# Linear attention and a gated mixture product on one Trainium2 core: VectorE's reciprocals and x multiplications queued behind the features of later pairs

## The chip, the core and the metric

The kernel runs on one core of a Trainium2 chip. Times are device microseconds (us) of one execution; the figure of a kernel is the median of its runs. The engines are TensorE (PE in the views, with its weight loads as PEld), VectorE (DVE), ScalarE (ACT), GpSimd (POOL) and SyncE (SP), which issues all DMA transfers of this kernel. Each engine works through its own instruction queue in order.

## The reference

```python
def phi(x):
    proj = x @ w_phi                                   # 64 -> 128 features
    proj = proj - max(abs(proj), axis=-1)
    return concatenate([exp(proj), exp(-proj)])        # 256
q_p, k_p = phi(q), phi(k)
kv = k_p.T @ v                                         # per batch and head
z = sum(k_p over tokens)
num, den = q_p @ kv, q_p @ z + 1e-6
x = (num / den), heads side by side                    # 4608 tokens x 512
out = ((x @ w_a) * (x @ w_b)) @ w_out                  # 512 -> 1536 -> 512
```

8 batches, 8 heads, 576 tokens, head size 64; all in float32.

## The kernel before

**Attention** goes over 32 pairs of heads (4 for each of 8 batches). For one pair, K is projected to features in two halves of two token chunks (`features`: TensorE makes pk, VectorE takes the maximum m, L228, and subtracts it into kd, L229; ScalarE takes the exponentials), a remainder chunk is shared by two pairs, and K's features are multiplied with V into kv. The query side makes e0 and e1, and `numerators` multiplies them with kv: the numerators go to DRAM as xun, the denominators as den. `reciprocals` loads the denominators back in another layout (r, 128 x 9), adds EPS (L394), takes the reciprocal (L395) and stores it as rec in DRAM.

**The mixture** works on blocks of 512 tokens; blocks 0 to 8 of the first pass, with 4 of 12 slices of the inner 1536 columns, run beside attention. `x_chunk` loads 128 rows of the numerators (x32) and the reciprocals, spread over 64 rows each (rb, two buffers), and VectorE multiplies them (L583). `load_x` splits the result into xh and xl, and `moe_block` makes, for each of four slices, pa and pb on TensorE (L626, 24 matmuls), h = pa * pb on VectorE (L631), its split hh and hl, and at the end the output product po (L647, 48 matmuls): 144 matmuls a block. Blocks 7 and 8 need the last batch and run after attention, beside the decoding of the weights of the second pass (`decode`, L453 to L459, `load_factors`), whose matmuls (`winograd`, L721) follow block 8. Chunk c of block j needs pair 4b + c, where b is the batch that holds the block's last token.

**Order.** `attention_steps` plans every step of a pair at a turn (4 turns from pair to pair after the first 7, 5 before); steps are traced turn by turn, and between the turns `run` traces steps of the mixture at PACE steps a turn. That is program order. The scheduler then fixes each engine's order with a time model of its own: an instruction goes when its inputs are ready by that model, the earliest in program order first. So instructions whose inputs the model takes for ready can go ahead of earlier ones. A block's multiplications, traced when its four pairs are long done, thus stand one by one in VectorE's queue, each soon after its own pair's reciprocal. The chip keeps the order, whatever the real arrival times are.

Of the kernel before, what the change touches and what calls it, by code (L numbers as in the profile page):

```python
# [13 lines left out]
ALU = mybir.AluOpType  # L14
# [4 lines left out]
P = 128  # L19
EPS = 1e-6  # L20


TURNS0, TURNS, PAIRS0 = 5, 4, 7
# [7 lines left out]
Q_TURNS, Q_STEP, NUM_TURN, QB, PB, Q32 = (4, 6), 2, 12, 2, 2, 3  # L31


DECODE_TURN, X_LAG, BLOCK_LAG = 2, 2, 8
PACE0, PACE, PACE0_UNTIL = 0.6, 0.62, 18


# [22 lines left out]
def tile_kernel(ctx, tc, qT, km, kr, vm, vr, w_phi, w_a, w_b, w_out, out):  # L60
# [13 lines left out]
    nc = tc.nc  # L74
    B, H, _, S = qT.shape
    NPAIR = H // 2
    D, F = w_phi.shape
# [29 lines left out]
    def products(a, b):  # L107

        if len(a) == 1:
            return [(a[0], b[0])]  # L110
        return [(a[0], b[0]), (a[0], b[1]), (a[1], b[0])]
# [32 lines left out]
    def engine(step, b):  # L144
        return {"v": nc.vector, "s": nc.scalar}[ENGINES[step][min(b, 2)]]
# [7 lines left out]
    def split(hi, lo, src, eng_hi, eng_lo):  # L153

        copy(eng_hi, hi, src)
        eng_lo.tensor_tensor(lo, src, hi, op=ALU.subtract)  # L156

    def stack(hi_lo, src, eng_hi, eng_lo):

        copy(eng_hi, hi_lo, src)  # L160
        eng_lo.tensor_tensor(hi_lo[D:], src[D:], hi_lo[D:], op=ALU.subtract)

    def k_load(b, pr, a1, a2, ps, consts, st):
        vaug = consts[-1]
        u = f"{b}_{pr}"
        i = b * NPAIR + pr
        n = NFULL * P
        k32 = a1.tile([P, n], F32, tag="k32", bufs=2, name=f"k32_{u}")
        nc.sync.dma_start(k32, km[b, pr])
        if i < PLAIN_KV:  # L170
            v32 = a1.tile([P, NFULL, 2, D + 1], F32, tag="vl", bufs=2, name=f"v32_{u}")
            nc.vector.memset(v32[:, :, :, D : D + 1], 1.0)
        else:
            v32 = a1.tile([P, NFULL, 2, D], F32, tag="v32", name=f"v32_{u}")
        nc.sync.dma_start(v32[:, :, :, :D], vm[b, pr])
        yield
        st["k", b, pr] = (k32,)
        if i >= PLAIN_K:
            kh, kl = (a1.tile([P, n], F32R, tag=f"k{p}", bufs=2, name=f"k{p}_{u}") for p in "hl")
            split(kh, kl, k32, engine("k_hi", b), engine("k_lo", b))  # L180
            st["k", b, pr] = (kh, kl)
        yield
        st["v", b, pr] = (v32,)
        if i >= PLAIN_KV:
            va = vaug[pr % 2]
            vl = a1.tile([P, NFULL, 2, D + 1], F32R, tag="vl", bufs=2, name=f"vl_{u}")
            split(va[:, :, :, :D], vl[:, :, :, :D], v32, engine("v_hi", b), engine("v_lo", b))
            st["v", b, pr] = (va, vl)
        yield
# [25 lines left out]
    def features(u, i, k_, c0, n, a2, ps, consts):  # L215

        wk32, wks = consts[3:5]
        d = a2.tile([P, 4, F], F32, tag="kd", bufs=2, name=f"kd_{u}")[:, : 2 * n]
        pk = ps.tile([P, 2, 2 * F], F32, tag="att", name=f"pk_{u}")
        parts = products(k_, (wk32,) if len(k_) == 1 else wks)  # L220
        for c in range(n):
            tok = slice((c0 + c) * P, (c0 + c + 1) * P)
            for n_, (x_, w_) in enumerate(parts):
                at = dict(start=(c == n_ == 0), stop=(n_ == len(parts) - 1))
                nc.tensor.matmul(pk[:, c], x_[:, tok], w_, skip_group_check=True, **at)
        p = pk[:, :n].rearrange("p c (j f) -> p (c j) f", j=2)
        m = a2.tile([P, 4], F32, tag="m", name=f"m_{u}")
        nc.vector.tensor_reduce(out=m[:, : 2 * n], in_=p, op=ALU.max, axis=AX.X, apply_absolute_value=True)  # L228
        nc.vector.tensor_tensor(d, p, m[:, : 2 * n].unsqueeze(2).broadcast_to([P, 2 * n, F]), op=ALU.subtract)  # L229
        yield  # L230
        plain = i < PLAIN_KV
        shape = [P, 2 * n, 2, F]
        if plain:
            e = a2.tile(shape, F32, tag=f"keh{n}", bufs=n, name=f"ke_{u}")
        else:
            e = a2.tile([P, 4, 2, F], F32, tag="ke", bufs=2, name=f"ke_{u}")[:, : 2 * n]
        nc.scalar.activation(e[:, :, 0, :], d, AF.Exp)  # L237
        nc.scalar.activation(e[:, :, 1, :], d, AF.Exp, scale=-1.0)
        es = (e,)
        if not plain:  # L240
            eh = a2.tile(shape, F32R, tag=f"keh{n}", bufs=n, name=f"keh_{u}")
            el = a2.tile(shape, F32R, tag=f"kel{n}", bufs=n, name=f"kel_{u}")
            split(eh, el, e, engine("ke_hi", i // NPAIR), nc.vector)
            es = (eh, el)
        yield es
# [16 lines left out]
    def rest_chunk(b, g, a1, a2, ps, consts, st):  # L262

        gen = features(f"{b}_{g}_r", b * NPAIR + 2 * g, st["rk", b, g], 0, 1, a2, ps, consts)
        yield next(gen)
        st["re", b, g] = next(gen)
        yield
# [121 lines left out]
    def reciprocals(b, pr, a1):  # L389
        n = 2 * S // P  # L390
        hs = slice(2 * pr, 2 * pr + 2)
        r = a1.tile([P, n], F32, tag="rec", bufs=2, name=f"r_{b}_{pr}")
        nc.sync.dma_start(r, den[b][hs].rearrange("h (a n) -> (h a) n", n=n))
        nc.vector.tensor_scalar_add(r, r, EPS)  # L394
        nc.vector.reciprocal(r, r)  # L395
        nc.sync.dma_start(rec[b][hs].rearrange("h (a n) -> (h a) n", n=n), r)
        yield

    def attention_steps(pools, consts, st):

        stages, x_first = [], first_block_x()

        def plan(unit, turns):
            for t in turns:
                stages.append((t, len(stages), unit))

        for i in range(B * NPAIR):
            b, pr = divmod(i, NPAIR)
            t0 = TURNS0 * min(i, PAIRS0) + TURNS * max(i - PAIRS0, 0)
            plan(k_load(b, pr, *pools, consts, st), [t0 + t for t in LOAD_TURNS])  # L410
            if pr % 2 == 0:
                plan(rest_load(b, pr // 2, *pools, consts, st), [t0 + t for t in REST_LOAD_TURNS])
            for c0 in range(0, NFULL, 2):
                plan(k_chunks(b, pr, c0, *pools, consts, st), [t0 + K_STEP * c0 // 2 + t for t in K_TURNS])
            if pr % 2 == 0:
                plan(rest_chunk(b, pr // 2, *pools, consts, st), [t0 + t for t in REST_TURNS])
            plan(rest_add(b, pr, st), [t0 + REST_ADD_TURNS[pr % 2]])
            plan(k_finish(b, pr, *pools, consts, st), [t0 + t for t in KV_TURNS])
            plan(q_project(b, pr, *pools, consts, st), [t0 + t for t in PROJECT_TURNS])
            for j in range(2):  # L420
                plan(q_side(b, pr, j, *pools, consts, st), [t0 + Q_STEP * j + t for t in Q_TURNS])
            plan(numerators(b, pr, *pools, consts, st), [t0 + NUM_TURN])
            plan(reciprocals(b, pr, pools[0]), [t0 + NUM_TURN])
            if b == 0:
                plan(x_first, [t0 + NUM_TURN + X_LAG])
            if pr == NPAIR - 1:
                plan(b, [t0 + NUM_TURN])
        stages.sort(key=lambda x: x[:2])
        for turn, group in itertools.groupby(stages, key=lambda x: x[0]):
            ready = None  # L430
            for _, _, unit in group:
                if isinstance(unit, int):
                    ready = unit
                else:
                    next(unit, None)
            yield turn, ready
# [130 lines left out]
    def x_chunk(j, c, pool):  # L567

        T, u = TS[0], f"0_{j}"
        x32 = pool.tile([P, T], F32, tag="x32", bufs=NCC, name=f"x32_{u}_{c}")  # L570
        rb = pool.tile([P, T], F32, tag="rb", bufs=2, name=f"rb_{u}_{c}")

        t = j * T
        while t < (j + 1) * T:
            b, s0 = divmod(t, S)
            n = min(S - s0, (j + 1) * T - t)
            src, dst = slice(s0, s0 + n), slice(t - j * T, t - j * T + n)
            nc.sync.dma_start(x32[:, dst], xun[b][c * P : (c + 1) * P, src])
            for i in range(2):
                h = 2 * c + i  # L580
                nc.sync.dma_start(rb[i * D : (i + 1) * D, dst], rec[b][h : h + 1, src].broadcast_to([D, n]))
            t += n
        nc.vector.tensor_tensor(x32, x32, rb, op=ALU.mult)  # L583
        return x32

    def load_x(j, pool):
# [6 lines left out]
    def first_block_x():  # L593

        for x_ in load_x(0, xpool):
            first_x.append(x_)
            yield
# [404 lines left out]
    with ExitStack() as c:  # L1002
        pools = attention_pools(c)
# [129 lines left out]
```

## Time and profile before

| | |
|---|---|
| median of 3 runs | 1243.63 us (1243.04 to 1245.67) |
| the profiled execution, whole time | 1245.73 us |
| its span, first to last instruction | 1243.9 us |
| TensorE busy | 1193.5 us (96%) |
| VectorE busy | 1003.8 us (81%) |
| ScalarE busy | 631.7 us (51%) |
| mean granted TensorE clock | 0.995 |

A busy share is a mean over stages: attention with the mixture blocks fills the first half of the span, the second and third pass of the mixture the rest. A matmul's end is modelled, so its shown duration (about 0.4 us for 512 columns) overlaps the next ones; the step from start to start is the pace.

### The profile page before, as it was taken

The numbers are of one execution on the slowest core, as the hardware profiler recorded it, in microseconds if no ns is written. First come the engines' busy times: TensorE is split into PE (matmuls) and PEld (weight loads), VectorE is DVE, ScalarE is ACT, GpSimd is POOL, SyncE is SP. The second block draws the span as 40 slices with busy tenths as digits, with TensorE's granted clock in tenths as the row PEclk, the third lists the DMA queues.
The fourth block names the chain that finished last, engine by engine and source line by source line (L and its number), as shares of the span: only waits on it lengthen the run. The fifth ranks groups of instructions, "written<-read, shape, count | busy, mean of one in ns | idle before, by whom it ended". The sixth has DMA issues, their size and how long they took to land.

```text
span 1243.9 us, 18463 instructions
## 1 busy us (share of the span) xinstructions
PE 1193.5 (96%) x6533; PEld 935.6 (75%) x6533; DVE 1003.8 (81%) x1715; ACT 631.7 (51%) x1236; POOL 159.4 (13%) x68
## 2 busy tenths in 40 slices
PE   7888999999999999989999999999999999999997
PEld 4455767776777777777678888878788888888887
DVE  6999978787887979866398865888897688888686
ACT  5756756665665656746254444343444243434332
POOL 2332223231332313312000000000000000000000
PEclk9999999999999999999999999999999999999999
DMA  6665444453442535422373241747489714241312
GB/s 206 192 198 164 123 139 135 120 160 104 152 145 90 172 102 158 133 75 99 97 249 115 98 122 32 242 153 244 152 296 387 250 51 152 68 157 64 127 69 84
DMA packets 129788, 182.84 MB, mean 147 GB/s; under 512 B 35488, under 2 KB 64672, under 8 KB 129696
## 3 DMA queue, kind: packets, MB, share of 16 engines
q1 hardware_dynamic: 129696, 181.67, 45.5%
q8 instruction: 51, 0.84, 0.3%
q14 instruction: 41, 0.34, 0.1%
HBM read 123.06 MB, written 58.56 MB: 146 GB/s over the span
## 4 chain that ended last, share of the span: by engine, by line
PE 44%; DVE 27%; DMA 20%; issue 4%; ACT 3%; SPq 2%; DVEq 0%; ACTq 0%
PE pba L721 6%; PE paa L721 6%; PE po L933 5%; PE po L647 4%; PE pb L626 4%; DMA rb<-rec 4%; PE poa L826 3%; PE pa L626 3%; DMA rec<-r 3%; PE pac L721 3%; PE pbc L721 3%; DMA r<-den 2%; DVE qs L338 2%; PE kvps L281 2%; DVE kel L156 2%
## 5 line engine op out<-in xcount | busy, mean ns | idle before, releaser
L351 POOL PARTITION_ALL_REDUCE mb<-p x64 | 159.2, 2507 | 424.3 <-ACT p L344 330.5
L355 ACT ACTIVATE qe<-p 128x576 f32<-128x576 f32 x64 | 44.0, 687 | 60.4 <-DVE p L352 46.1
L371 PE MATMUL pn<-qe,kvh 128*64 128x288 f32 x512 | 71.9, 414 | 1.4 <-ACT qe L355 0.8
L156 DVE TENSOR_TENSOR kel<-ke,keh 128x1024 fp32r<-128x1024 f32 x50 | 63.0, 1262 | 9.3 <-ACT keh L149 9.0
L237 ACT ACTIVATE ke<-kd 128x512 f32<-128x512 f32 x64 | 40.6, 634 | 50.2 <-DVE kd L229 49.6
L626 PE MATMUL pb<-xh,w_b_h 128*128 128x512 f32 x144 | 58.6, 407 | 7.5 <-DVE h L631 6.8
L647 PE MATMUL po<-hh,w_o_h 128*128 128x512 f32 x144 | 57.6, 407 | 5.2 <-DVE h L631 4.4
L647 PE MATMUL po<-hl,w_o_h 128*128 128x512 f32 x144 | 57.8, 403 | 1.8 <-DVE hl L156 1.7
L626 PE MATMUL pa<-xh,w_a_h 128*128 128x512 f32 x144 | 57.6, 400 | 1.6 <-DVE xh L151 1.5
L149 ACT CAST hh<-h 128x512 fp32r<-128x512 f32 x36 | 22.4, 622 | 72.4 <-DVE h L631 72.3
L626 PE MATMUL pa<-xl,w_a_h 128*128 128x512 f32 x144 | 57.3, 398 | 1.1 <-DVE xl L156 1.1
L583 DVE TENSOR_TENSOR x<-x,rb 128x512 f32<-128x512 f32 x36 | 25.9, 719 | 40.1 <-DMA rb<-rec 37.2
L626 PE MATMUL pb<-xl,w_b_h 128*128 128x512 f32 x144 | 57.5, 399 | 0.0
L626 PE MATMUL pb<-xh,w_b_l 128*128 128x512 f32 x144 | 57.3, 398 | 0.0
L647 PE MATMUL po<-hh,w_o_l 128*128 128x512 f32 x144 | 57.1, 398 | 0.0
L281 PE MATMUL kvps<-keh,vaug 128*65 128x256 f32 x200 | 56.6, 283 | 0.5 <-ACT keh L149 0.4
L626 PE MATMUL pa<-xh,w_a_l 128*128 128x512 f32 x144 | 56.9, 395 | 0.0
L371 PEld LDWEIGHTS pn<-qe,kvh 128*64 128x64 f32 x512 | 34.4, 136 | 29.8 <-issue 5.5
L933 PE MATMUL po<-hl,w_o_h 128*128 128x512 f32 x144 | 56.3, 391 | 0.0
L281 PE MATMUL kvps<-kel,vaug 128*65 128x256 f32 x200 | 56.2, 281 | 0.0
L281 PE MATMUL kvps<-keh,vl 128*64 128x256 f32 x200 | 56.1, 280 | 0.0
L933 PE MATMUL po<-hh,w_o_l 128*128 128x512 f32 x144 | 56.1, 389 | 0.0
(331 smaller groups left out, 3689.3 us busy)
## 6 DMA issues: line engine op xcount, KB each, us to landing
x<-xnorm SPq DMA_DIRECT2D x32, 512.0 KB
o<-part SPq DMA_DIRECT2D x61, 256.0 KB
q<-in_qT SPq DMA_DIRECT2D x108, 144.0 KB
xun<-xn SPq DMA_DIRECT2D x32, 288.0 KB
xnorm<-x SPq DMA_DIRECT2D x36, 256.0 KB
part<-o SPq DMA_DIRECT2D x18, 512.0 KB
part<-o SPq DMA_DIRECT2D x36, 256.0 KB
k<-in_km SPq DMA_DIRECT2D x32, 256.0 KB
```

Of the source, the lines that this page charges most:

```text
L156: eng_lo.tensor_tensor(lo, src, hi, op=ALU.subtract)
L237: nc.scalar.activation(e[:, :, 0, :], d, AF.Exp)
L281: nc.tensor.matmul(st["kv_ps", b, pr][:width, j], v_[:, j, :width], e_[:, j], start=(left == NFULL and j == 0 and n_ == 0), stop=(left == ...
L351: nc.gpsimd.partition_all_reduce(mb, p32, P, bass_isa.ReduceOp.absmax)
L355: nc.scalar.activation(e[:, 0], p32, AF.Exp)
L371: nc.tensor.matmul(pn[j * D : (j + 1) * D, :HALF], kv[:, 2 * j + s, :D], e[:, s, tok], **at)
L583: nc.vector.tensor_tensor(x32, x32, rb, op=ALU.mult)
L626: nc.tensor.matmul(acc, w[:, cc * P : (cc + 1) * P], x, start=(k == 0), stop=(k == 3 * NCC - 1))
L647: nc.tensor.matmul(acc, w[:, cc * P : (cc + 1) * P], h, start=(k == 0), stop=(k == 3 * NFS[p] - 1))
L721: nc.tensor.matmul(accs[to][i], w_, x_, skip_group_check=True, **at)
L826: nc.tensor.matmul(accs[to][m], w_, x_, skip_group_check=True, **flags)
L933: nc.tensor.matmul(acc[key], w[:, cc * P : (cc + 1) * P], h[:, tok], skip_group_check=True, **n_)
```

## The change

Two kinds of VectorE instructions get edges that set their place in VectorE's queue, without a wait on any result. The addition in front of the reciprocal of pair i goes behind the subtraction kd of pair i + 3, second half. The multiplication of chunk c of a block goes behind the kd of pair + 4, first half, where pair is the one that the chunk needs last. Only kd from pair 7 on are used. Where there are no four later pairs (blocks 7 and 8), the multiplication is kept behind the VectorE instruction traced just before it. In program order, the addition is traced three turns after the denominators' reload, and the first block's x one turn later.

```diff
-DECODE_TURN, X_LAG, BLOCK_LAG = 2, 2, 8
+DECODE_TURN, X_LAG, BLOCK_LAG = 2, 3, 8
...
+    behind = {}
+
+    def placed(i, c0, op):
+
+        if i >= PAIRS0 and (i + c0[0], c0[1]) in behind:
+            with tc.issue_after(behind[i + c0[0], c0[1]]):
+                return op()
+        return op()
...
-        nc.vector.tensor_tensor(d, p, m[:, : 2 * n].unsqueeze(2).broadcast_to([P, 2 * n, F]), op=ALU.subtract)
+        kd = nc.vector.tensor_tensor(d, p, m[:, : 2 * n].unsqueeze(2).broadcast_to([P, 2 * n, F]), op=ALU.subtract)
+        if n == 2:
+            behind[i, c0] = kd.ins
...
         nc.sync.dma_start(r, den[b][hs].rearrange("h (a n) -> (h a) n", n=n))
-        nc.vector.tensor_scalar_add(r, r, EPS)
+        yield
+        placed(b * NPAIR + pr, (3, 2), lambda: nc.vector.tensor_scalar_add(r, r, EPS))
         nc.vector.reciprocal(r, r)
...
-            plan(reciprocals(b, pr, pools[0]), [t0 + NUM_TURN])
+            plan(reciprocals(b, pr, pools[0]), [t0 + NUM_TURN + t for t in (0, 3)])
...
-        nc.vector.tensor_tensor(x32, x32, rb, op=ALU.mult)
+        multiply = lambda: nc.vector.tensor_tensor(x32, x32, rb, op=ALU.mult)
+        pair = ((j + 1) * T - 1) // S * NPAIR + c
+        if pair + 4 < B * NPAIR:
+            placed(pair, (4, 0), multiply)
+        else:
+            tc.keep_in_program_order(multiply())
         return x32
```

## Rows read from the trace of the kernel before

**Rows 1.** Windows: us from:to, length, then busy us of each engine.

```profile
core 0: us, PE busy (x) PEld busy (x) DVE busy (x) ACT busy (x) POOL busy (x), PEclk, DMA share, GB/s
165.00:575.00 410.00, 392.42 (x2577) 301.54 (x2576) 338.10 (x534) 253.88 (x522) 108.92 (x42) 0.99 0.42 128
```

**Rows 2.** Groups by line, VectorE, 165 to 575 us: busy, mean ns, idle before.

```profile
L583 DVE TENSOR_TENSOR x<-x,rb 128x512 f32<-128x512 f32 x21 | 15.6, 744 | 30.3 <-DMA rb<-rec 27.9 <-issue 2.3
L394 DVE TENSOR_SCALAR r<-r 128x9 f32<-128x9 f32 x22 | 4.8, 220 | 32.7 <-DMA r<-den 32.7
```

**Rows 3.** The page's chain that ended last, shares by engine.

```profile
PE 44%; DVE 27%; DMA 20%; issue 4%; ACT 3%; SPq 2%; DVEq 0%; ACTq 0%
```

**Rows 4.** Waits of TensorE, 165 to 575 us: us in total, times, longest.

```profile
PE pb L626 <- DVE h L631: 6.8, 5, 2.4
PE po L647 <- DVE h L631: 3.5, 1, 3.5
PE pq L343 <- DVE qs L338: 3.4, 2, 1.9
PE po L647 <- DVE hl L156: 1.7, 3, 0.6
PE pa L626 <- DVE xh L151: 1.3, 1, 1.3
PE pq L343 <- DVE rkh L151: 0.6, 1, 0.6
```

**Rows 5.** Timeline of VectorE, 297 to 320 us: start, length, idle time before.

```profile
297.92 0.17 DVE L394 TENSOR_SCALAR r<-r 128x9 f32<-128x9 f32 x1 [2.31 <-DMA r<-den]
...
303.04 0.69 DVE L583 TENSOR_TENSOR x<-x,rb 128x512 f32<-128x512 f32 x1 [4.70 <-DMA rb<-rec]
303.65 0.69 DVE L631 TENSOR_TENSOR h<-pb,h 128x512 f32<-128x512 f32 x1
...
307.52 0.68 DVE L229 TENSOR_TENSOR kd<-pk,m 128x512 f32<-128x512 f32 x1
...
319.66 0.69 DVE L229 TENSOR_TENSOR kd<-pk,m 128x512 f32<-128x512 f32 x1
```

**Rows 6.** Timeline of TensorE around the same stall.

```profile
302.05 0.28 PE L281 MATMUL kvps<-keh,vaug 128*65 128x256 f32 x1
304.39 0.50 PE L626 MATMUL pb<-xh,w_b_h 128*128 128x512 f32 x1 [2.07 <-DVE h L631]
```

**Rows 7.** Windows where the granted clock (PEclk) falls, and right after.

```profile
460.30:463.70 3.40, 3.19 (x8) 2.52 (x9) 3.40 (x7) 1.10 (x2) 0.00 (x0) 0.50 0.36 135
463.70:467.10 3.40, 3.40 (x23) 2.78 (x23) 3.37 (x8) 2.73 (x5) 0.00 (x0) 1.00 0.42 117
552.45:555.86 3.41, 3.41 (x12) 2.65 (x12) 3.38 (x6) 3.41 (x8) 0.00 (x0) 0.50 0.64 210
```

**Rows 8.** Timeline of SP's queue, 298 to 301 us.

```profile
298.37 0.32 SPq L396 DMA_DIRECT2D rec<-r  x1
299.77 1.12 SPq L581 DMA_DIRECT2D rb<-rec  x2
```

**Rows 9.** Timeline of VectorE: last chunk of blocks 1 and 6, and kd four pairs on.

```profile
170.96 0.69 DVE L583 TENSOR_TENSOR x<-x,rb 128x512 f32<-128x512 f32 x1 [4.83 <-DMA rb<-rec]
...
187.10 0.68 DVE L229 TENSOR_TENSOR kd<-pk,m 128x512 f32<-128x512 f32 x1
...
563.24 0.69 DVE L583 TENSOR_TENSOR x<-x,rb 128x512 f32<-128x512 f32 x1 [0.92 <-DMA rb<-rec]
...
573.39 0.69 DVE L229 TENSOR_TENSOR kd<-pk,m 128x512 f32<-128x512 f32 x1
```

**Rows 10.** Timeline where block 8 begins: TensorE (PE), and VectorE's decoding (DVE).

```profile
652.22 0.39 PE L647 MATMUL po<-hh,w_o_h 128*128 128x512 f32 x1
...
654.32 0.39 PE L626 MATMUL pa<-xh,w_a_h 128*128 128x512 f32 x1
...
668.51 0.43 DVE L457 TENSOR_SCALAR w_1q_a<-w_1q_a 128x512 uint32<-128x512 uint32 x1
```

**Rows 11.** Timeline of TensorE at the first matmul of block 4.

```profile
414.69 0.28 PE L225 MATMUL pk<-wkh,kl 128*128 128x256 f32 x1
...
415.33 0.40 PE L626 MATMUL pa<-xh,w_a_h 128*128 128x512 f32 x1
```

## The prediction

> **What bounds the kernel now.** I first read the windows of the busy times. From 165 to 575 us, where attention and the mixture blocks run side by side, TensorE is busy for 392.4 of 410 us and VectorE for 338.1 [rows 1]. So TensorE is nearly full, and VectorE has 71.9 us of idle time. The groups by line say where that idle time sits: 32.7 us before the 22 additions of EPS (L394, the first step of a reciprocal), all of it until the reload of the denominators landed, and 30.3 us before 21 multiplications of x (L583), 27.9 of it until the spread reciprocals landed [rows 2]. That is 63.0 of 71.9 us: VectorE stands almost only at the two instructions which the change moves.
>
> Does that idle time set the end? The chain that ended last runs 20% through transfers and 27% through VectorE [rows 3], but a chain follows one path and says nothing of the next one behind it. So I read TensorE's own waits in the same stretch [rows 4]. They add up to 6.8 + 3.5 + 3.4 + 1.7 + 1.3 + 0.6 = 17.3 us, all six of them on VectorE, and 410 - 392.4 = 17.6 us is all the idle time that TensorE has there. The two timelines show how one leads to the other: VectorE stands 4.70 us before x at 303.04 [rows 5], issues the product h (L631) behind it, and TensorE, which needs the PSUM buffer that h is made from, stands 2.07 us until 304.39 [rows 6]. VectorE's stall of 4.7 us costs TensorE 2.1, since the rest is covered by matmuls that don't depend on it.
>
> **What is removed.** Of TensorE's waits I credit those on h, qs and xh to the moved instructions, as VectorE's queue is late there by what it stood before: 6.8 + 3.5 + 3.4 + 1.3 = 15.0 us in 9 waits. Those on hl and rkh (2.3 us) I leave out: hl also waits for ScalarE. The upper bound is 17.3. Two smaller terms go with them. A matmul's modelled end hides part of each wait: 302.05 to 304.39 is 2.34 us, the usual step to the next issue in that run of matmuls is about 0.12, so 2.2 are lost where 2.07 are shown; 9 times 0.15 is 1.4 us. And twice the granted clock halves behind such waits: 0.50 in the stretches from 460.30 and from 552.45, against 1.00 right after [rows 7]; these are its levels of 1.2 and 2.4 GHz. Both follow a wait on h (one the longest of all, 3.5 us). Half of 3.4 us is lost each time, 3.4 us together. The gain is 15.0 + 1.4 + 3.4 = 19.8 us, with bounds of 0 (the stalls come back elsewhere) and 17.6 + 1.4 + 3.4 = 22.4 us.
>
> **Are the stalls gone where the instructions go?** Take pair 14. Its addition stands at 297.92; the features three pairs later, second half (kd of pair 17), are subtracted at 307.52, and those of pair 18, first half, at 319.66 [rows 5]. The reload landed when the addition began, so 9.6 us later it has long landed: no wait. Its multiplication goes behind 319.66, 12 us behind the new place of the reciprocal. The way between them is the store of rec, which SP issues at 298.37, and the two loads of rb from 299.77 on [rows 8], landed at 303.04: 5.1 us from the addition's start. So about 7 us of margin remain for SP's queue. The transfers move too: rec's store waits on SP for the later reciprocal, and whatever SP issues behind it (loads of k, v and q for later pairs) waits with it; SP's order is planned with the same edges, so I price this at 0, up to the 30.3 us of VectorE's stalls at x if the margin fails (a rival below). Nothing is removed from VectorE's work: the same 36 multiplications and 32 reciprocals.
>
> **What is added, first: x comes later.** Pinned behind the features four pairs on, the last chunk of a mixture block's x moves from 170.96 to behind 187.10 for block 1, and from 563.24 to behind 573.39 for block 6 [rows 9]; read so for blocks 1 to 6, the six delays add to 50.7 us. The block's first matmuls need x. A block has 144 matmuls, at 0.233 us (nine from 652.22 to 654.32 [rows 10]) 33.6 us, and one comes each 78.5 us (170.96 to 563.24 is five blocks), so a block fills 43% of TensorE's time. If TensorE lost that share in all the delays, 21.8 us: the upper bound; the lower one is 0, as attention's own matmuls can come forward. I take 2: TensorE already runs the projection of the features in question (pk, 414.69) just ahead of the block's first matmul (pa, 415.33) [rows 11], so only the chain behind pk (maximum, subtraction, multiplication, split, some 4 us) is new, and as the blocks run one after the other without a pause, the delay is paid once: 43% of 4 us.
>
> **Second: the last two blocks.** Their eight multiplications are kept in program order. For block 7 this means behind block 6's last h, while block 6's output product of 48 matmuls (11.2 us) still runs: hidden. Block 8 is traced after the decoding of the next weights has been given 27 steps (nine and two rounds of 2.5). A matrix pair takes 11 steps, so the 27th is the fifth step of the third, and x of block 8 stands behind its second L457, at 668.51, while TensorE now begins block 8 at 654.32 [rows 10]. 14.2 us late; block 7 has 48 - 9 = 39 output matmuls left to cover 9.1 of them. That leaves 5 us, as the four multiplications leave the stretch before that place and have to be done behind it. Bounds: 0, if the decoding comes forward with the earlier end of attention, and 14.2, if nothing covers it. I take 5.
>
> **Third: the first block.** X_LAG puts its x one turn later in program order and the reciprocals of all pairs three turns; pairs 0 to 6 have no pin. A turn is 78.5 / 16 = 4.9 us, of which 43% would be lost if block 0 moved by it: 2 us; the lower bound is 0, and I take 1. The additions of the last three pairs (29 to 31) have no pin either, and I expect their stalls to stay.
>
> **The sum.** -19.8 + 2 + 5 + 1 = -11.8 us. The profiled execution took 1245.73 us in all, 1243.9 of it span; it would come to 1233.9. It lies 2.1 us above the median of the three runs shown, so against 1243.63 I forecast 1231.8, rounded 1232.
>
> One rule of the Trainium skill would give another sum. Its Perfetto Trace Analysis, section Identifying the Most-Contended Engine, says that matmul busy time is no good measure of TensorE's load and that the busy share of weight loads is a better one. By that reading TensorE is 301.5 / 410 = 74% loaded here [rows 1], VectorE at 82% is the engine to relieve, and its 63.0 us would come off in full: 1181. The waits of TensorE speak against it: of 63.0 us only 15 reach TensorE as idle time.
>
> **The rivals.**
> *VectorE is the bound, TensorE has room.* For it: weight loads fill 301.5 us of the 410 only [rows 1]. Against it: TensorE's idle time there is 17.6 us, its clock is granted at 0.99, and between waits it starts a 512-column matmul every 0.233 us. In full it gives 1243.6 - 63.0 = 1181; half of it 1212. Chance 0.07.
> *The stall moves to x.* The reciprocal and its multiplication are moved together; if SP's queue uses up the 7 us of margin, x stalls as now and only L394's 32.7 us go. Most of TensorE's waits are on h, which stands right behind x (303.04, 303.65 [rows 5]), so about half the gain is left: 9.9 - 8 = 2 us, 1242. Chance 0.15, 0.09 of it within 0.2%, which is about what a measurement of this kernel can tell from no change.
> *Slower: the blocks starve TensorE.* The late x leaves TensorE without block matmuls at each of six block starts, and attention can't come forward since its own chain through VectorE and ScalarE sets its pace. At 43% of 50.7 us: -19.8 + 21.8 + 5 + 1 = +8, 1252. It decides from a loss of 13.8 us, 27% of the delays. For it: delays as long as 16 us. Against it: VectorE gets 63 us back in that stretch, with which attention does come forward. Chance 0.17.
> *Nothing moves*, since the planner had that order already, is excluded: the places at 303.04 and 319.66 differ by 16.6 us.
>
> **How the numbers follow.** The forecast has 0.61: faster, by 11.8 us, and by itself 1224 to 1239 (costs of 0 and gains of 19.8; costs doubled and two gains of three). Faster by over 0.2%: 0.61 + 0.07 + 0.06 = 0.74; within it 0.09; slower 0.17. The range leaves out the fuller half of the first rival and the outer part of the third: 1218 to 1248.
>
> **What the profile of the changed kernel would show.** Right: idle time before the addition and x between 165 and 575 under 15 us together, TensorE's waits on h and qs there under 5, no half clock in that stretch, attention's last reciprocal earlier by over 10 us. A pause of TensorE of some 5 us where block 8 begins. Wrong: TensorE waiting for xh at the block starts (starved), idle time at x as before (moved), or new idle time of VectorE behind SP's queue. An order that the planner changes elsewhere, above all in the decoding of the weights, would make the sum wrong without any of these.

## The result and the profile after

Median of 4 runs 1228.59 us (1228.31 to 1231.36), the kernel before beside it 1244.65 us (4 runs, 1243.04 to 1247.42): a ratio of 0.9874, 95% interval 0.985 to 0.9898. The profiled execution took 1228.45 us in all (span 1226.7), 17.3 us less than the one before.

Windows of the changed kernel, columns as in [rows 1]:

```profile
165.00:575.00 410.00, 409.96 (x2735) 317.98 (x2737) 344.31 (x546) 271.68 (x548) 104.44 (x44) 1.00 0.44 130
575.00:630.00 55.00, 46.41 (x216) 33.74 (x215) 34.79 (x78) 19.84 (x42) 0.00 (x0) 0.94 0.57 185
612.53:619.36 6.83, 4.40 (x10) 3.18 (x11) 6.15 (x16) 3.72 (x9) 0.00 (x0) 0.50 0.92 299
```

From 165 to 575 us TensorE has no idle time left (409.96 of 410) and starts 2735 matmuls where it started 2577 [rows 1]. The view of TensorE's waits is empty there, against the six rows of [rows 4], and the granted clock is 1.00 throughout. Right behind it the picture turns: 8.6 us idle between 575 and 630, and 6.83 us at a granted clock of 0.50 (1.2 of 2.4 GHz).

Groups by line of VectorE, 165 to 575 us, which answer to [rows 2]:

```profile
L595 DVE TENSOR_TENSOR x<-x,rb 128x512 f32<-128x512 f32 x21 | 14.8, 706 | 4.2 <-DMA rb<-rec 3.4 <-DMA q<-in_qT 0.8
...
L406 DVE TENSOR_SCALAR r<-r 128x9 f32<-128x9 f32 x23 | 5.3, 231 | 3.0 <-DMA r<-den 3.0
```

The idle time at the two instructions fell from 63.0 to 7.2 us. VectorE's waits in the same stretch, largest first (what waits, for what: us in total, times, longest), show who is waited for now:

```profile
DVE h L648 <- PE pb L643: 21.9, 5, 7.4
DVE m L237 <- PE pk L234: 13.1, 11, 2.1
```

VectorE waits for TensorE, no longer TensorE for VectorE. Its idle time as a whole hardly fell, from 71.9 to 65.7 us (410 less its busy time): what changed is where it stands. The timeline around pair 14's multiplication, which stood 4.70 us in [rows 5]:

```profile
308.17 0.69 DVE L238 TENSOR_TENSOR kd<-pk,m 128x512 f32<-128x512 f32 x1
308.77 0.68 DVE L595 TENSOR_TENSOR x<-x,rb 128x512 f32<-128x512 f32 x1
```

It starts 0.6 us behind the kd that it is pinned to, with no idle time. The chain that ended last, to be held against [rows 3]:

```profile
PE 72%; DVE 15%; DMA 8%; ACT 2%; issue 2%; SPq 0%; DVEq 0%; ACTq 0%
```

Transfers have gone from 20% of it to 8%, VectorE from 27% to 15%, and TensorE from 44% to 72%.

**Where the time came from and where some went back.** I took landmarks on TensorE: the last po matmul of a block. Block 6 ends at 628.64 us before and at 603.88 after, 24.8 us earlier; block 8 ends at 696.78 and at 681.12, 15.7 us earlier; the whole execution is 17.3 us shorter. So some 9 us were given back between the ends of blocks 6 and 8. TensorE's timeline after, at the start of block 7, says where:

```profile
603.88 0.40 PE L664 MATMUL po<-hh,w_o_l 128*128 128x512 f32 x1
604.11 0.39 PE L643 MATMUL pa<-xh,w_a_h 128*128 128x512 f32 x1
...
608.80 0.51 PE L643 MATMUL pa<-xl,w_a_h 128*128 128x512 f32 x1 [1.26 <-DVE xl L156]
...
611.02 0.50 PE L643 MATMUL pa<-xh,w_a_h 128*128 128x512 f32 x1 [1.00 <-DVE xh L151]
...
614.96 0.79 PE L643 MATMUL pa<-xl,w_a_h 128*128 128x512 f32 x1 [3.22 <-DVE xl L156]
```

And VectorE's timeline, block 7's four multiplications and some of what stands between them:

```profile
592.59 0.69 DVE L156 TENSOR_TENSOR hl<-h,hh 128x512 fp32r<-128x512 f32 x1 [0.69 <-ACT hh L149]
593.20 0.69 DVE L595 TENSOR_TENSOR x<-x,rb 128x512 f32<-128x512 f32 x1
596.07 0.43 DVE L466 TENSOR_SCALAR w_1q_a<-w_1q_a 128x512 uint32<-128x512 uint32 x1 [2.18 <-ACT w_1q_a L465]
...
597.95 0.68 DVE L595 TENSOR_TENSOR x<-x,rb 128x512 f32<-128x512 f32 x1
...
603.38 0.68 DVE L595 TENSOR_TENSOR x<-x,rb 128x512 f32<-128x512 f32 x1
603.98 0.68 DVE L541 TENSOR_TENSOR w_1q_a<-w_1q_a 128x512 f32<-128x512 f32 x1
...
608.67 0.68 DVE L595 TENSOR_TENSOR x<-x,rb 128x512 f32<-128x512 f32 x1
```

The first stands behind the last split of block 6's h, the others some 5 us apart, with splits, the decoding of weights and work on the second pass's x in between. The last one comes 16.1 us behind hl and 4.6 us behind the block's first matmul. The matmuls of the first slice trickle until 615.55, with 5.5 us of shown waits, and the 6.83 us at the lower clock (612.53 to 619.36) begin during the longest of these waits.

### The profile page after: what moved, and what is told of

Same layout as the page of the kernel before. It is cut to its first block, busy times and chain, and to the rows that moved or that the text cites. A ratio compares the mean times of both kernels' runs of the same rounds, so it can differ in the third digit from the quotient of the medians.

```text
span 1226.7 us, 18458 instructions
## 1 busy us (share of the span) xinstructions
PE 1189.7 (97%) x6533; PEld 935.2 (76%) x6533; DVE 999.2 (81%) x1715; ACT 636.7 (52%) x1236; POOL 150.0 (12%) x68
## 4 chain that ended last, share of the span: by engine, by line
PE 72%; DVE 15%; DMA 8%; ACT 2%; issue 2%; SPq 0%; DVEq 0%; ACTq 0%
PE kvps L292 8%; PE pb L643 8%; PE po L664 7%; PE pa L643 7%; PE pba L738 6%; PE paa L738 6%; PE po L950 5%; PE pn L382 4%; PE pk L234 3%; PE poa L843 3%; PE pac L738 3%; DMA x<-xnorm 3%; PE pbc L738 3%; PE pd L391 2%; PE pq L354 2%
## 5 line engine op out<-in xcount | busy, mean ns | idle before, releaser
L362 POOL PARTITION_ALL_REDUCE mb<-p x64 | 149.8, 2362 | 409.1 <-ACT p L355 248.1
L156 DVE TENSOR_TENSOR kel<-ke,keh 128x1024 fp32r<-128x1024 f32 x50 | 67.6, 1354 | 7.0 <-ACT keh L149 6.0
L363 DVE TENSOR_TENSOR p<-p,mb 128x576 f32<-128x576 f32 x64 | 60.6, 947 | 2.4 <-POOL mb L362 2.0
L149 ACT CAST keh<-ke 128x1024 fp32r<-128x1024 f32 x50 | 52.4, 1047 | 13.5 <-PE kvps L292 13.3
L237 DVE TENSOR_REDUCE m<-pk 128x4 f32<-128x512 f32 x64 | 43.8, 684 | 16.3 <-PE pk L234 16.1
```

Source lines behind the costliest of these rows:

```text
L149: eng.copy(dst, src)
L362: nc.gpsimd.partition_all_reduce(mb, p32, P, bass_isa.ReduceOp.absmax)
L363: engine("q_sub", b).tensor_tensor(p32, p32, mb, op=ALU.subtract)
```

## The experiments

Theory: VectorE's two stalls for reloads set TensorE's pace from 165 to 575 us; the pins remove them; what is given back is the pin of the last two blocks. Rivals: the later program order does it, without the pins; one kind of instruction alone carries the gain; the shift of x costs TensorE its block matmuls; the idle time of VectorE is only a companion, not the cause. Ratios are to the kernel before on the same chip. Matmuls are those that TensorE started from 165 to 575 us, and idle is VectorE's before the additions and x in that stretch; both come from the windows and the groups by line, as above.

| kernel | median, us | ratio (95%) | idle, us | matmuls |
|---|---|---|---|---|
| before | see text | 1 | 63.0 | 2577 |
| changed | 1228.59 | 0.9874 (0.985 to 0.9898) | 7.2 | 2735 |
| reciprocals only | 1227.46 | 0.9831 (0.9796 to 0.9866) | 24.6 | 2722 |
| x only | 1230.61 | 0.9851 (0.9819 to 0.9883) | 23.4 | 2724 |
| turns only | 1249.53 | 1.0009 (0.999 to 1.0027) | 66.6 | 2583 |
| x beside the reciprocals | 1232.63 | 0.9866 (0.9826 to 0.9906) | 23.1 | 2715 |
| last blocks unpinned | 1227.4 | 0.9798 (0.975 to 0.9846) | 15.3 | 2732 |
| x five pairs on | 1248.72 | 0.9976 (0.9952 to 1.0) | 2.1 | 2654 |
| extra additions, unpinned | 1241.08 | 0.9919 (0.9889 to 0.9949) | 63.2 | 2615 |
| extra additions, pinned | 1229.34 | 0.9833 (0.9798 to 0.9868) | 12.7 | 2727 |
| changed, again | 1231.96 | 0.985 (0.9823 to 0.9877) | 8.6 | 2727 |
| last blocks unpinned, again | 1225.0 | 0.9799 (0.9772 to 0.9826) | 15.6 | 2733 |
| block 7 unpinned | 1225.06 | 0.9804 (0.9777 to 0.9832) | 15.7 | 2727 |
| block 8 unpinned | 1231.68 | 0.9856 (0.9829 to 0.9883) | 7.4 | 2727 |

The kernel before took 1244.65 us beside the changed one and 1248.25, 1249.54 and 1249.67 us on the chips of the three sets of experiments, in that order.

### One part alone

Reciprocals only: x's multiplications as before, no pin and no kept order; the later turns stay.

```diff
-        if pair + 4 < B * NPAIR:
-            placed(pair, (4, 0), multiply)
-        else:
-            tc.keep_in_program_order(multiply())
+        nc.vector.tensor_tensor(x32, x32, rb, op=ALU.mult)
```

> Only the reciprocals are pinned (and traced three turns later); the multiplications of x float as in the kernel before, those of blocks 7 and 8 too. Theory (VectorE's stalls delay TensorE): VectorE's idle time before the addition of EPS is gone between 165 and 575 us, that before x stays at 20 to 30 us, TensorE's waits there fall from 17.3 to 8 to 12 us, and block 7 begins without a pause: 1230 to 1238. Rival (the planner's new order made the gain, not the stalls): no tie to the idle time before x, the time is that of the full change or that of before, within 3 us.

x only: the addition and its turn as before, X_LAG 2 again.

```diff
-        yield
-        placed(b * NPAIR + pr, (3, 2), lambda: nc.vector.tensor_scalar_add(r, r, EPS))
+        nc.vector.tensor_scalar_add(r, r, EPS)
...
-            plan(reciprocals(b, pr, pools[0]), [t0 + NUM_TURN + t for t in (0, 3)])
+            plan(reciprocals(b, pr, pools[0]), [t0 + NUM_TURN])
```

> Only x's multiplications are pinned (those of blocks 7 and 8 kept in program order); the reciprocals float as before. Theory: VectorE's idle time before x falls from 30 to under 6 us, that before the addition stays near 33, TensorE's waits up to 575 us fall to 3 to 8, and the pause at block 7 (some 9 us) is there: 1232 to 1240. Rival (the order, not the stalls): the time of the full change or of before, within 3 us.

Turns only: both instructions without a pin, the later turns and X_LAG 3 kept.

```diff
-        placed(b * NPAIR + pr, (3, 2), lambda: nc.vector.tensor_scalar_add(r, r, EPS))
+        nc.vector.tensor_scalar_add(r, r, EPS)
...
-            placed(pair, (4, 0), multiply)
+        nc.vector.tensor_tensor(x32, x32, rb, op=ALU.mult)
```

> No pins at all: only the tracing three turns later of the reciprocals, and one turn later of the first block's x. Theory: program order alone moves nothing that is ready in the planner's model; idle time at both places as before (over 50 us of 63), time within 4 us of before. Rival (the gain is the program order's): over half of the gain, under 1236.

Groups by line of VectorE, 165 to 575 us, with the reciprocals alone pinned:

```profile
L595 DVE TENSOR_TENSOR x<-x,rb 128x512 f32<-128x512 f32 x23 | 17.5, 761 | 19.0 <-DMA rb<-rec 16.5 <-issue 2.5
...
L406 DVE TENSOR_SCALAR r<-r 128x9 f32<-128x9 f32 x23 | 5.1, 223 | 5.6 <-DMA r<-den 5.4
```

The same with x alone pinned:

```profile
L594 DVE TENSOR_TENSOR x<-x,rb 128x512 f32<-128x512 f32 x21 | 15.4, 731 | 3.6 <-DMA rb<-rec 2.3 <-DMA q<-in_qT 1.3
...
L405 DVE TENSOR_SCALAR r<-r 128x9 f32<-128x9 f32 x23 | 5.7, 247 | 19.8 <-DMA r<-den 19.8
```

The turns alone do nothing (1.0009, stalls 66.6 us): the pins do it. But each part alone brings nearly the whole gain, which I had not expected: the stall of the instruction without a pin shrinks too (x from 30.3 to 19.0 us, the addition from 32.7 to 19.8), and TensorE's waits in the stretch come to 0.8 and 0.3 us, although VectorE still stands 24 us. One thing must be kept apart: reciprocals only leaves blocks 7 and 8 unpinned too, so it is to be held against the last blocks unpinned (0.9798 and 0.9799), not against the changed kernel; x only keeps that pin. From the end of block 0 to the end of block 6 TensorE needs 462.6 us before, 440.7 with the last blocks unpinned (second set) and 442.1 with the reciprocals alone: these bring 20.5 of 21.9 us. It needs 438.0 us in the changed kernel and 439.1 with x alone: x brings 23.5 of 24.6 us. Why a pin on the one shortens the stall of the other was not followed up.

### Other distances

x beside the reciprocals: the multiplication goes behind the same kd as its own pair's addition (three pairs on, second half), half a pair nearer to its reciprocal.

```diff
-            placed(pair, (4, 0), multiply)
+            placed(pair, (3, 2), multiply)
```

> The full change, but x's multiplications are pinned behind the same kd as the pair's reciprocal (three pairs on, second half) instead of the next pair's: the 12 us between them fall to what the planner puts there. TensorE's order differs from the full change in few places. Theory: the stall comes back before x, 2 to 5 us at most of the 21, 40 to 80 us on VectorE, TensorE waits for h again, 1235 to 1245. Rival (the order made the gain): within 3 us of the full change, 1226 to 1232.

The stall at x rose from 4.2 to 18.3 us, far less than expected, and TensorE's waits to 2.1 us. The interval of the time holds the changed kernel's, so this run does not tell the theory from its rival; it agrees with the two above, in that a stall of some 20 us costs TensorE little.

x five pairs on: a pair further than the change, where there is one.

```diff
-        if pair + 4 < B * NPAIR:
+        if pair + 5 < B * NPAIR:
+            placed(pair, (5, 0), multiply)
+        elif pair + 4 < B * NPAIR:
             placed(pair, (4, 0), multiply)
```

> The full change with x pinned behind the first features five pairs on instead of four: about 17 to 20 us later for each chunk. Rival of the prediction (late x starves TensorE at the start of a block): TensorE waits for xh at the starts of blocks 2 to 6 and is slower than the full change by over 5 us. Theory (attention comes forward and fills, since TensorE is full either way): within 3 us of the full change up to the end of block 6.

Nearly the whole gain is gone (0.9976), though VectorE's stalls are smaller than ever (2.1 us), and TensorE's waits in the stretch come to 2.5 us. Its windows row for 165 to 575 us:

```profile
165.00:575.00 410.00, 407.41 (x2654) 308.06 (x2653) 338.53 (x539) 267.82 (x539) 112.89 (x44) 1.00 0.44 130
```

81 matmuls less than in the changed kernel, behind a PE column that looks full. TensorE's timeline at the end of one block and the start of the next, at two places (only the blocks' matmuls are shown):

```profile
254.35 0.40 PE L666 MATMUL po<-hh,w_o_l 128*128 128x512 f32 x1
258.81 0.40 PE L645 MATMUL pa<-xh,w_a_h 128*128 128x512 f32 x1
...
329.43 0.39 PE L666 MATMUL po<-hh,w_o_l 128*128 128x512 f32 x1
335.23 0.40 PE L645 MATMUL pa<-xh,w_a_h 128*128 128x512 f32 x1
```

4.5 and 5.8 us pass here between two blocks, in which only attention's matmuls run; over the five starts of blocks 2 to 6 it is 22.0 us, in the changed kernel 7.6, in the kernel before 7.1. Block 6 ends at 616.7 us instead of 603.9, which is about what the profiled execution, 1240.11 us, is longer by (11.7). It is the fastest of ten; the other nine took 1243.83 to 1251.57 us at mean granted clocks of 0.987 to 0.993, against its 0.995, so the profile does not show the whole loss of the median. So a place one pair further on loses what the prediction's slower rival feared to lose. That late blocks starve TensorE is not shown, though: in the first of these pauses attention's matmuls follow one another at their usual pace,

```profile
256.70 0.28 PE L292 MATMUL kvps<-keh,vaug 128*65 128x256 f32 x1
256.81 0.28 PE L292 MATMUL kvps<-kel,vaug 128*65 128x256 f32 x1
256.93 0.28 PE L292 MATMUL kvps<-keh,vl 128*64 128x256 f32 x1
```

0.12 us from start to start, so TensorE does not stand between the blocks; its planned order has attention's matmuls there. Of the 12 us, 2.5 are shown waits, none of them on xh or xl; where the rest goes, behind modelled ends that overlap, stays open.

### Is the idle time the cause?

The stall brought back by other instructions: for each pair two additions that nothing uses, each with a reload of its own (rx reads the denominators, ry what rx stored). First unpinned, traced where the reload is:

```diff
+        def add_x():
+            nc.vector.tensor_scalar_add(rx, rx, EPS)
+            nc.sync.dma_start(rows(spare_rec), rx)
+            nc.sync.dma_start(ry, rows(spare_rec))
+        def add_y():
+            nc.vector.tensor_scalar_add(ry, ry, EPS)
...
+        nc.sync.dma_start(rx, rows(den))
+        add_x()
+        add_y()
```

> The full change and two more additions for each pair, with no use: one on a second copy of the denominators, one on a copy of its result that has gone through DRAM and back. Both float, as the reciprocal and x did in the kernel before. They cost VectorE under 0.5 us a pair of work. Theory (TensorE loses what VectorE stands, once that exceeds what its queue can bear): VectorE's idle time rises again to 50 to 100 us between 165 and 575, TensorE waits for h, qs and xh, and the gain is lost: 1238 to 1255. Rival (the order made the gain): within 4 us of the version with the same additions pinned.

Then the same additions and transfers, pinned as the change pins its own:

```diff
+        placed(i, (3, 2), add_x)
+        yield
+        placed(i, (4, 0), add_y)
```

> The same as the run before, with the same two additions, but both pinned: the first behind the features three pairs on, the second behind those of four. Theory: VectorE's idle time before them under 10 us, time within 5 us of the full change (the added work and transfers are hidden), and 8 us or more under the version that lets them float. Rival (the added work or transfers cost by themselves): slower than the full change by as much as the floating version.

Groups by line, VectorE, 165 to 575 us, unpinned:

```profile
L409 DVE TENSOR_SCALAR rx<-rx 128x9 f32<-128x9 f32 x21 | 4.9, 234 | 24.4 <-DMA rx<-den 24.4
...
L414 DVE TENSOR_SCALAR ry<-ry 128x9 f32<-128x9 f32 x21 | 4.3, 206 | 33.1 <-DMA ry<-spare 33.0
```

and pinned:

```profile
L409 DVE TENSOR_SCALAR rx<-rx 128x9 f32<-128x9 f32 x23 | 5.4, 235 | 0.3 <-DMA rx<-den 0.3
...
L414 DVE TENSOR_SCALAR ry<-ry 128x9 f32<-128x9 f32 x22 | 4.1, 184 | 2.4 <-DMA ry<-spare 2.4
```

Same work, same transfers, 1241.08 against 1229.34 us on one chip: 11.7 us hang on where the additions stand. With 63.2 us of stalls back in VectorE's queue, TensorE's waits are back too (13.2 us in the stretch), and so is the old rate of matmuls for the most part (2615). What the additions cost by themselves, pinned, is small: 1229.34 us against 1227.4 with the last blocks unpinned, on the same chip. That is the fair comparison, and not the changed kernel (0.9874), since neither run with extra additions has the pause at block 7: TensorE waits for no xh or xl there, pinned or not. What is not clean: the place in program order differs as well, so the planned orders of the two differ somewhat beyond the additions.

### What was given back

Last blocks unpinned, run in two sets:

```diff
         else:
-            tc.keep_in_program_order(multiply())
+            multiply()
```

> The full change, but the multiplications of blocks 7 and 8 float instead of being kept in program order. TensorE's order differs in few places. Theory (that pin costs the pause at block 7: 24.7 us gained up to the end of block 6, 15.7 left at the end of block 8): TensorE's waits on xl and xh at block 7 and the half clock behind them go, 6 to 9 us under the full change, 0.980 to 0.983 of before. Rival (the pause is owed to the decoding of the weights that starts there): within 2 us of the full change.

> The full change with the multiplications of blocks 7 and 8 floating. Theory: the pause at block 7 (waits on xl and xh and the half clock, together some 7 to 9 us) is gone and nothing takes its place: 4 to 9 us under the full change on the same chip. Rival: what block 7 gives back is lost again in the later passes: within 2 us.

The changed kernel itself beside the second of these, with no edit:

> The full change once more, to be compared on one chip with the three versions beside it: 0.985 to 0.990 of before.

And each of the two blocks alone (here block 7 unpinned; the other run has `j == 7` and unpins block 8):

```diff
         else:
-            tc.keep_in_program_order(multiply())
+            ins = multiply()
+            if j == 8:
+                tc.keep_in_program_order(ins)
```

> Only block 7 floats, block 8 stays in program order. Theory (block 7's pin costs the pause; block 8's is covered): as the version with both floating, within 2 us. The prediction's own step (block 8 behind the decoding of the weights, 5 us) would have it slower than that by 5 us.

> Only block 8 floats, block 7 stays in program order. Theory: the pause at block 7 stays, and the time is that of the full change within 2 us. The prediction's own step would have it 5 us faster.

All four of the last set on one chip: 1231.96 us with both pins, 1231.68 without block 8's, 1225.06 without block 7's, 1225.0 without either. Block 7's pin costs 6.9 us, block 8's nothing. TensorE's waits from 600 to 632 us agree. Without block 8's pin:

```profile
PE pa L645 <- DVE xl L156: 4.6, 2, 3.6
PE pb L645 <- DVE h L650: 2.0, 1, 2.0
PE po L666 <- ACT o L668: 1.6, 1, 1.6
PE pa L645 <- DVE xh L151: 1.4, 1, 1.4
```

Without block 7's pin none is on xl or xh:

```profile
PE pa L645 <- ACT o L668: 1.5, 1, 1.5
PE po L666 <- ACT o L668: 0.8, 2, 0.6
PE pb L645 <- ACT h L649: 0.7, 1, 0.7
```

Windows of the version without either, at the place of the pause:

```profile
600.00:632.00 32.00, 29.62 (x124) 22.73 (x123) 29.80 (x65) 16.10 (x34) 0.00 (x0) 1.00 0.79 263
```

against the changed kernel's:

```profile
600.00:632.00 32.00, 25.11 (x96) 18.64 (x95) 28.63 (x62) 11.76 (x25) 0.00 (x0) 0.89 0.73 238
```

28 matmuls more in the same 32 us, at 0.233 us each 6.5 us of work: the 6.9 us of the medians within their spread. The pin on block 7's multiplications is the loss, and the version without it beats both kernels, 2.0% below the kernel before. The pin by itself need not cost: with the extra additions pinned it is there as well, but the last of block 7's multiplications starts 0.1 us behind the block's first matmul (611.70 and 611.63 us), against 4.6 us in the changed kernel, and no wait on xh or xl comes of it.

## Why the prediction was right, and where it was not

Forecast 1232 us, measured 1228.59: faster, for the reason given. Step by step, with the profiled executions:

**The bound.** Right. VectorE stood only at the two instructions, and through h this reached TensorE. The two runs with extra additions show that the idle time is the cause. The first rival (VectorE is the bound, 1181 us) is out: of 63.0 us that VectorE stood, 24.8 came off up to the end of block 6. The rule on which it leaned, of the Trainium skill's Perfetto Trace Analysis, section Identifying the Most-Contended Engine, judges TensorE's headroom by MFU (the share of its peak arithmetic) and by the busy share of weight loads, of which the prediction used the second. The trace differs from the room that the prediction read out of it: after the change that share is 318 / 410 = 78% with no idle time shown, and 77 to 78% in each run with 7 to 25 us of such stalls (316 to 319 us), so in this stretch the missing 22% were no room. As a measure of change the share does better than the busy time of matmuls: with x five pairs on it falls to 308.1 us, by 9.9, where the matmuls' busy time falls by 2.6.

**The gain, 19.8 us with 22.4 as its upper bound, was mis-sized: it measured 24.8.** All 17.6 us of shown idle time went, the 2.3 us on hl and rkh too, which I had left out, and both stretches at half clock (3.4). These are 21.0. The other 3.8 I had as 1.4, what modelled ends hide in 9 waits. The stretch from 575 us to the end of block 6, which I didn't count, holds next to nothing of it: 1.8 us of idle time before, 1.7 in the changed kernel. 0.2 us come from before block 0's end. How the rest divides was not measured. The count of matmuls says about the same without modelled ends: 158 more, at 410 / 2735 = 0.15 us each, are 23.7 us of work (an estimate, since they are not all of one size).

**No stall where the instructions go.** Right: 7.2 us remain (foreseen: under 15). SP's queue did not use up the 7 us of margin, so the rival in which the stall moves to x is out. It would have been nearly as fast all the same: the reciprocals alone, with 19.0 us of stalls left at x, gain 20.5 of 21.9 us up to the end of block 6, as read above. This is the rival's own step that was wrong: it took TensorE's loss to fall in proportion to the stalls that go, and it does not.

**Late x at blocks 1 to 6, 2 us.** Measured at most 0.5: no wait of TensorE on xh or xl there, and the pauses between blocks at the starts of blocks 2 to 6 add to 7.6 us, 7.1 before. Attention does come forward, as argued. The margin is under one pair: five pairs on, nearly the whole gain is lost.

**The last two blocks, 5 us at block 8 and block 7 hidden.** This step failed, in place and in size. Block 8 goes on from block 7 without a pause (637.72, 637.96 and so on to 638.65, in steps of 0.23 us), and unpinning it changes nothing. Block 7 pays: some 9 us in the profiled execution, 6.9 in medians. The step had counted that block 6's output product covers 11.2 us behind its last h, and had not counted that kept order holds each of the four multiplications behind what is traced just before it: the last one comes 16.1 us behind hl. The question to ask was not when the first may go but when the last does. Its bounds (0 to 14.2) held the size, for another place and another reason.

**The first block, 1 us.** Block 0 ends at 166.1 us before and 165.9 after: 0.

**The sum.** -24.8 + 9.1 - 1.6 = -17.3 us, for -11.8. The 1.6 us come off behind block 8, where nothing of the change lies, and are no gain: the stretch behind block 8 takes 547.2 us before and 545.5 after, but 552.1 and 545.0 in the two profiled executions of the version with the last blocks unpinned. The errors of the gain (5.0 too small) and of the pin (4.1 too small) nearly cancel; the 3 us of costs at the late x and the first block, which did not arise, and these 1.6 make up nearly all of the 5.5 us between the two sums. That the forecast lay so near is in part due to this, which is luck. Its own range does not follow as written: costs doubled together with two thirds of the gain would end at 1246, not 1239; either alone ends near 1239.

**The signs in the profile.** Waits on h and qs under 5 us: none. No half clock in the stretch: none. Attention's last reciprocal earlier by over 10 us: it stands here,

```profile
589.13 0.17 DVE L406 TENSOR_SCALAR r<-r 128x9 f32<-128x9 f32 x1 [4.84 <-DMA r<-den]
589.34 0.22 DVE L407 RECIPROCAL r<-r 128x9 f32<-128x9 f32 x1
```

25.5 us before its old place (614.87). The stalls of pairs 29 to 31, which have no pin, stayed, as the 4.84 us above. A pause at block 8: none, it was at block 7.

## What to carry to other kernels

An instruction that waits for a value on its way through DRAM should stand in its engine's queue where the value has long landed; pin it behind work that comes well over one round trip later (here the two pins of pair 14 stand 15.3 us apart, at 292.85 and 308.17 us, for a trip of 5.1 us), but not much further, since one pair more lost nearly the whole gain here. When an instruction is kept behind its predecessor in program order, follow the last of the group, not the first, to its consumer. To see what a stall costs, count the matmuls that start in a stretch, since a busy column with modelled ends can look full while 81 of them are missing.

## What the runs showed that was not expected

**A queue's stalls cost little up to a point.** x five pairs on aside, with 7 to 25 us of such stalls of VectorE in 410 us, TensorE starts 2715 to 2735 matmuls, a spread of 20 or 3 us of work; with 63 to 67 us, 2577 to 2615. The stalls' price is not proportional; no run lies between 25 and 63 us, so where it begins is open.

**One program, different stretches at half clock.** The changed kernel's second profiled execution, which need not be on the chip of the first, has a span of 1231.6 us against 1226.7. Two pairs of windows, in the first execution:

```profile
79.32:82.73 3.41, 2.37 (x15) 1.55 (x14) 3.07 (x8) 3.41 (x8) 0.30 (x1) 1.00 0.83 218
82.73:86.14 3.41, 2.69 (x15) 1.49 (x16) 3.41 (x4) 1.00 (x4) 3.41 (x2) 1.00 0.60 197
...
628.87:632.28 3.41, 3.41 (x16) 2.77 (x15) 3.38 (x8) 0.38 (x2) 0.00 (x0) 1.00 0.00 0
632.28:635.69 3.41, 3.41 (x17) 2.72 (x16) 3.41 (x9) 2.62 (x6) 0.00 (x0) 1.00 0.52 154
```

and in the second:

```profile
79.32:82.73 3.41, 1.49 (x9) 1.06 (x10) 2.65 (x6) 3.41 (x8) 0.00 (x0) 1.00 0.34 110
82.73:86.14 3.41, 3.41 (x12) 2.78 (x12) 2.47 (x3) 2.58 (x8) 2.13 (x1) 0.50 0.91 245
...
628.87:632.28 3.41, 1.46 (x6) 1.05 (x6) 3.41 (x8) 1.82 (x4) 0.00 (x0) 1.00 0.00 1
632.28:635.69 3.41, 3.41 (x9) 2.67 (x8) 2.88 (x6) 0.54 (x1) 0.00 (x0) 0.50 0.05 8
```

Where the second execution has TensorE busy for 1.49 and 1.46 us only, the granted clock is 0.50 in the next stretch (1.2 GHz), where the first has 1.00 (2.4 GHz). The half clock behind block 7's waits is in both (from 612.53 and from 615.21 us, 6.83 us each). So a gain of a few us that rests on a stretch's clock in a single profile is not yet a gain of the kernel. This holds for the 3.4 us counted above: the granted clock from 165 to 575 us is 0.99 with the turns only, as before, but 1.00 with the extra additions unpinned, which have 13.2 us of waits.
